# The run-in of an adaLN attention and MLP block: layer norm evicted unmodulated from two PSUM tensors, modulated in SBUF, K in two parts, later loads held back

## The chip, the cores and the metric

The kernel runs on one core of one Trainium2 chip. The metric is the device time of one execution in microseconds (us). The engines named below are PE (matrix multiply), ACT (ScalarE), DVE (VectorE), POOL (GpSimd) and SP, which here only issues transfers. A change of under 0.3% (2.35 us of 782.72) is about what a measurement of this kernel cannot tell from no change: the three runs shown lie 2.65 us apart.

## The reference

One block of 2048 tokens of width 512 with adaptive layer norm: six vectors come from a condition `c`, and modulate the input of a 32-head attention and of a GELU MLP.

```python
mod = (_silu(c) @ w_mod).reshape(c.shape[0], 6, 1, -1)
sa, ca, ga, sb, cb, gb = (mod[:, 0], mod[:, 1], ..., mod[:, 5])
h = _layernorm(x, axis=-1) * (1 + ca) + sa
x = x + ga * _A_ref(h, A_wqkv, A_wo)     # softmax(q k^T / 4) v per head of 16, then @ wo
h = _layernorm(x, axis=-1) * (1 + cb) + sb
x = x + gb * _B_ref(h, B_w1, B_b1, B_w2, B_b2)   # gelu(h @ w1 + b1) @ w2 + b2
```

Shapes: x (1, 2048, 512), wqkv (512, 1536), wo (512, 512), w1 (512, 1376), w2 (1376, 512), c (1, 512), w_mod (512, 3072), all bfloat16.

## The kernel before

**Tiling.** The tokens form four blocks of 512 (`QB`), each of four tiles of 128. A block is normalised (`layer_norm`: statistics by `stats`, `z` by `apply`), its `z` is transposed by PE through the identity into PSUM, and evicted into `blk` (also called h) while scale and shift `modA` are applied (`modulate`, lines 667 to 674). From h come K (`make_k`, into `kT`), V (`make_v`, into `VEB`) and Q (`make_q`, into `qm`), 128 columns (eight heads) at a time. `rs` holds variance plus EPS; no version here takes a root of it, so that step costs the same in both.

**Attention.** The work is cut into 32 runs: a block of queries and four heads (at the end, half a block of queries and eight heads). A run goes over 16 key tiles of 128 keys; one key tile has four units of 512 columns, one for each 32-row group of PE. There are two ways to take the exponential of a key tile:

- On ACT (`qk_a`): PE writes scores into the PSUM tensors `st3` (three units) and `st2` (two) in turn, ACT exponentiates 128x1536 or 128x1024 at once into `pt` (line 943).
- On DVE (`qk_d`): PE writes one unit into `ax`, DVE turns it into int16 bits `ph` (line 984), and four shifted copies `sh` are made of a whole key tile (lines 1000 and 1016; POOL takes some quarters of the last one, line 1022). PE then multiplies five readings with five scaled copies of V (`VEB`, `VX`).

Each run has 12 own key tiles for ACT and 4 shared ones that DVE takes; but where ACT runs out of own tiles before DVE has begun a shared one, ACT takes it (`next_tile`). Run 0 has one shared tile. So the number of tiles of each kind comes out of the order.

**Order.** The whole order of every engine is written by a planner (`class Plan`) when the kernel is built. Each operation has an engine, a planned duration, dependencies and a priority; the planner picks, step by step, the ready operation with the best priority, with a small term drawn from `SEEDS`, one number for each 12.5 us of planned time. Where PE would stand idle it puts in "heat": a 128x512 matmul on a zero tile `warm` (lines 466, 471 and 482), so that PE's clock stays up. On the chip each engine then goes through its list strictly in order.

**The run-in.** SP issues, in this order: x of block 0 in two halves (line 537), w_mod for the first modulation in two halves of 512 KB (line 547), 128 columns of the Q and K weights (line 557), x of block 1, 128 columns of the V weights, the rest of the three weights, x of blocks 2 and 3. The statistics of block 0 need x, the vector `modA` needs w_mod and the silu of c (`first_mod`, line 640, 32 matmuls, and an add on DVE, line 644). All 16 transposes of block 0 write into one PSUM tensor (`st3`), and DVE, ACT, DVE, DVE evict it with `modA` applied. Q and K of block 0 are written into a second PSUM tensor (`st2`), and evicted one after the other: Q half 0 on DVE, K on ACT, Q half 1 on DVE. In the profile each of these evictions begins only when the one before it has ended, on the other engine too. Then the first scores and exponentials follow. Blocks 1 to 3 are normalised between the exponentials of run 0.

**The end.** Blocks 0 to 2 get their output projection, second norm and MLP between the exponentials of the later runs; so does the first half of block 3. What follows the last exponential (`last_half`) is the second half of block 3.

Of the kernel before, what the change touches and what calls it, by code (L numbers as in the profile page):

```python
# [11 lines left out]
ACT = mybir.ActivationFunctionType  # L12
# [13 lines left out]
NPH = 5  # L26
# [37 lines left out]
SEEDS = (421, 872, 550, 568, 152, 412, 578, 215, 443, 644, 509, 573, 863, 621, 363, 765, 575, 623, 840, 572, 68, 536, 307, 910, 236, 857, 622, 26, 489, 196, 660, 895, 259, 934, 819, 96, 576, 477, 556, 345, 216, 481, 3, 336, 398, 276, 175, 772, 338, 592, 137, 10, 817, 569, 785, 228, 673, 798, 588, 808, 688, 864, 394, 776)  # L64
# [219 lines left out]
def kernel(  # L284
# [125 lines left out]

    APR = 32
# [128 lines left out]
    o_mod = op("NIL", None, 0.0, (), lat=0.0, prio=-2.0, acq=r_g)  # L540

# [3 lines left out]
    def load_mod(h):  # L545
        def go(o):
            nc.sync.dma_start(out=o_mod.tile[:, 4 * h:4 * h + 4, :].rearrange("p (j n) q -> p j (n q)", n=2),
                              in_=wm_src[:, 2 * h:2 * h + 2, 0:2 * D])
        return dma(go, (o_mod,), kb=420, prio=0.2 * h - 4.0)
    o_wm = {h: load_mod(h) for h in (0, 1)}  # L550
# [4 lines left out]
    def load_cols(i, lo, hi, prio):  # L555
        def go(o):
            nc.sync.dma_start(out=o_w[i].tile[:, :, lo:hi], in_=wq_src[:, :, i * D + lo:i * D + hi])
        return dma(go, (o_w[i],), kb=192 if lo == 0 else 340, prio=prio, n=1.2)
    o_w0 = {i: load_cols(i, 0, P, (-3.0, -2.8, -2.4)[i]) for i in range(3)}
    o_w1 = {}  # L560
    for b in range(1, NQ):
        o_x[b] = load_x(b)
        o_x[b].prio = 0.5 * b - 3.1
        o_w1[b - 1] = load_cols((1, 2, 0)[b - 1], P, D, 0.5 * b - 2.7)
# [73 lines left out]
    def first_mod(ps, j):  # L638
        for m in range(2 * NC):
            nc.tensor.matmul(out=ps[:, m:m + 1], lhsT=mod_cols(j)[:, m * P:(m + 1) * P], rhs=sc[:, j:j + 1],  # L640
                             start=(j == 0 and m == 0), stop=(j == NC - 1 and m == 2 * NC - 1))
    mm_A = chain([(lambda ps, j=j: first_mod(ps, j), 0.28) for j in range(NC)], [o_sc, o_mod], "modA", r_ax, [o_mod],
                 need=lambda j: o_wm[j // 2])
    o_mA = op("DVE", lambda o: nc.vector.tensor_tensor(out=modA, in0=mm_A.tile[:, 0:2 * NC], in1=plus, op=ALU.add),
              0.2, [mm_A] + o_plus, prio=0.0, rel=(mm_A,))

# [35 lines left out]
    def layer_norm(src, deps, mod, mod_dep, hold_z, alloc_h, engines, ps_res, kind, prio,  # L682
# [3 lines left out]
        new = kind == "in0"  # L686

        def stat(t):
            stats(ln, t, src(t))
            if new and t > 1:  # L690
                plus_eps(nc.vector, ln, 0 if t == 2 else t, t + 1)
        st = [op("DVE", lambda o, t=t: stat(t), 0.98 if new and t > 1 else 0.83, (deps[t], ln, after and after[t]),
                 prio=prio) for t in range(nt)]
        if new:
            rs = 3 * [op("POOL", lambda o: rstd(ln, 0, 3, True), 0.8, [st[2], o_mh], prio=0.0)]
            rs.append(op("POOL", lambda o: rstd(ln, 3, 4, True), 0.8, [st[3], o_mh], prio=0.0))
        else:
            rs = [x for i in range(nt // 2) for x in 2 * [op(
                "POOL", lambda o, i=i: rstd(ln, 2 * i, 2 * i + 2), 1.3, st[2 * i:2 * i + 2] + [o_mh], prio=0.0)]]
        z = op("NIL", None, 0.0, (rs[0], hold_z), lat=0.0, prio=0.0, acq=r_z)  # L700
        za = [op("DVE", lambda o, t=t: apply(ln, z, t, src(t)), 0.33, (z, rs[t]), prio=prio,
# [4 lines left out]
        if isinstance(ps_res, tuple):  # L706
            hold = op("NIL", None, 0.0, (), lat=0.0, prio=-1.0, acq=ps_res[0]) if new else None
            firsts = []
            parts = ((0, 1), (2,), (3,)) if hold is not None else ((0, 1), (2, 3))
            two = [None, None]  # L710
            for part in parts:
                for half in range(2):
                    def tr(o, half=half, part=part, prev=two[half]):
                        if prev is not None:
                            o.tile = prev.tile
                        elif hold is not None:
                            o.tile = hold.tile[:, half * QB:(half + 1) * QB]
                        o.ps = o.tile.bitcast(BF16)
                        for j in (2 * half, 2 * half + 1):
                            for t in part:  # L720
                                nc.tensor.transpose(
                                    out=o.ps[:, (j % 2) * QB + t * P:(j % 2) * QB + (t + 1) * P],
                                    in_=z.tile[:, t, j * P:(j + 1) * P], identity=ident)
                    one = op("PE", tr, len(part) * 2 * 0.0705, za[0:part[-1] + 1] + [o_id, two[half]],
                             lat=PEL, mode=("full", 0), kind=kind,
                             acq=None if two[half] is not None or hold is not None else ps_res[half], rel=(z,))
                    if two[half] is None:
                        firsts.append(one)
                    two[half] = one
            trs += two  # L730
            for half in range(2):
                one = two[half]
                for j in (2 * half, 2 * half + 1):
# [3 lines left out]
                        0.5 if e == "DVE" else 0.72, (one, mod_dep, h), prio=0.2, rel=(hold or firsts[half],)))  # L737
# [16 lines left out]

    o_h = {}
# [7 lines left out]
    def proj(b, w, cc, kind, acq, after=None, into=None):  # L763
        js = (0, 2, 1, 3) if b else (0, 1, 2, 3)
        return chain([(lambda ps, j=j: nc.tensor.matmul(  # L765
            out=ps[:, 0:QB] if into is None else into(), lhsT=w.tile[:, j, cc * P:(cc + 1) * P], rhs=o_h[b].tile[:, j, :],
            start=(j == js[0]), stop=(j == js[-1])), MM) for j in js],
# [807 lines left out]
```

## Time and profile before

| what | us |
|---|---|
| three runs | 780.78, 782.72, 783.43 |
| median | 782.72 |
| the profiled execution | 784.56 |
| its span, first to last instruction | 782.8 |
| first exponential begins, in the span | 17.06 |
| last exponential ends | 759.9 |
| exponentials on ACT (626) | 710.7 busy |

The span is counted from the first to the last instruction of the profiled execution; 1.8 us of its time lie outside it. "busy" is the time in which an engine executes. A group of instructions is named by line, engine, operation, output<-input. The chain of waits goes back from the last instruction, at each step to what released it.

### The profile page before, as it was taken

To read this page: it belongs to the slowest core of one execution; us is meant where nothing else is said; L and a number is where in the kernel's file an instruction comes from. 1 tells how busy PE (TensorE), PEld (TensorE's weight loads), DVE (VectorE), ACT (ScalarE), POOL (GpSimd) and SP (SyncE) were. 2 spreads that over 40 slices of the span, in tenths; PEclk is the share of its full clock that TensorE was granted. 3 is DMA by queue.
4 is the path that set the end of the run, shared out by engine and by line. 5 is a ranking of instruction groups with operands and counts; after the bars stand their busy time and mean duration, and the time that the engine had idled before them with its cause. 6 is when DMAs were issued, how large, how long until landed. Compare 5 with 4: busy or idle time off the path is not lost.

```text
span 782.8 us, 20830 instructions
## 1 busy us (share of the span) xinstructions
PE 729.6 (93%) x8267; PEld 270.1 (35%) x8349; DVE 720.3 (92%) x1270; ACT 751.2 (96%) x676; POOL 256.8 (33%) x497
## 2 busy tenths in 40 slices
PE   7889999999999989999998999999999999989997
PEld 3333333233332323333222233222334444434454
DVE  5879988999999999999999999999889999999984
ACT  2999999999999999999999999999999999999994
POOL 4432433433345345232323114333122142322330
PEclk9999999999999999999999999999999999999999
DMA  6043011000011101010101000100011001001100
GB/s 215 28 120 109 19 24 43 20 9 19 23 44 52 26 20 46 13 23 12 43 21 22 29 19 24 22 20 26 26 47 32 20 24 46 17 12 31 26 18 28
DMA packets 35091, 27.71 MB, mean 35 GB/s; under 512 B 17941, under 2 KB 28726, under 8 KB 34994
## 3 DMA queue, kind: packets, MB, share of 16 engines
q1 hardware_dynamic: 34986, 26.39, 12.2%
q8 instruction: 65, 1.06, 0.6%
q14 instruction: 32, 0.26, 0.1%
q10 hardware_dynamic: 8, 0.00, 0.0%
HBM read 20.77 MB, written 2.61 MB: 30 GB/s over the span
## 4 chain that ended last, share of the span: by engine, by line
PE 39%; ACT 33%; DVE 14%; issue 10%; DMA 3%; SPq 1%; DVEq 0%; ACTq 0%
ACT pt L943 31%; PE od L1082 13%; PE st L894 11%; DVE ph L984 5%; DVE sh L1000 4%; PE ax L1248 4%; PE ax L894 3%; PE ax L1309 2%; PE ax L765 2%; DMA dc<-dn 1%; DMA g<-in_w_mod_dram 1%; PE ax L812 1%; DVE sh L1016 1%; PE t L1419 1%; ACT g L1324 1%
## 5 line engine op out<-in xcount | busy, mean ns | idle before, releaser
L943 ACT ACTIVATE pt<-st 128x1536 bf16<-128x1536 f32 x626 | 710.7, 1325 | 5.6 <-PE st L894 4.5
L984 DVE TENSOR_SCALAR ph<-ax 128x512 int16<-128x512 f32 x484 | 316.9, 682 | 21.7 <-PE ax L894 18.7
L894 PE MATMUL st<-qm,kT 32*128 32x512 bf16 x1564 | 247.0, 385 | 24.0 <-ACT pt L943 16.5
L1000 DVE TENSOR_SCALAR sh<-ph 128x2048 int16<-128x2048 int16 x363 | 241.2, 694 | 3.2 <-PE od L1082 2.0
L1022 POOL TENSOR_TENSOR sh<-ph,pair_sh 128x256 int32<-128x256 int32 x234 | 142.6, 616 | 265.4 <-DVE sh L1000 188.8
L1082 PE MATMUL od<-sh,VX 128*32 128x512 bf16 (+1 forms) x2432 | 171.2, 340 | 4.1 <-DVE sh L1000 2.3
L894 PE MATMUL ax<-qm,kT 32*128 32x512 bf16 x484 | 162.9, 379 | 4.7 <-DVE ph L984 2.6
L894 PEld LDWEIGHTS <-kT 32*128 32x128 bf16 x2048 | 79.8, 91 | 240.3 <-issue 228.7
L1082 PE MATMUL od<-pt,VEB 128*32 128x512 bf16 (+1 forms) x1952 | 142.7, 341 | 0.0
L1082 PEld LDWEIGHTS <-VEB 128*32 128x32 bf16 x2560 | 62.4, 96 | 74.6 <-issue 61.6
L1082 PEld LDWEIGHTS <-VX 128*32 128x32 bf16 x2432 | 59.3, 95 | 82.9 <-issue 72.3
L1134 POOL TENSOR_TENSOR OT<-OD,RB 128x256 bf16<-128x256 f32 x38 | 28.4, 753 | 103.4 <-DVE sh L1000 51.5
L1016 DVE TENSOR_SCALAR sh<-ph 128x2048 int16<-128x2048 int16 (+3 forms) x85 | 48.3, 577 | 1.8 <-PE od L1082 1.7
L1082 PE MATMUL od<-ph,VEB 128*32 128x512 bf16 (+1 forms) x608 | 47.7, 340 | 0.5 <-DVE OD L1107 0.5
L1309 PE MATMUL ax<-blk,W 128*128 128x512 bf16 (+1 forms) x152 | 41.2, 351 | 2.1 <-issue 0.8
L1248 PE MATMUL ax<-w,g 128*128 128x512 bf16 x114 | 32.3, 381 | 2.5 <-ACT g L1319 1.0
L828 POOL TENSOR_SCALAR VX<-VEB 128x128 bf16<-128x128 bf16 x64 | 23.9, 373 | 31.0 <-DVE VEB L680 28.0
L765 PE MATMUL ax<-blk,w 128*128 128x512 bf16 x93 | 31.0, 382 | 2.8 <-issue 0.6
L1314 DVE TENSOR_SCALAR g<-ax,b1c 128x512 bf16<-128x512 f32 (+1 forms) x44 | 29.4, 677 | 1.2 <-PE ax L1309 0.7
L1134 POOL TENSOR_TENSOR OS<-OD,RB 128x256 bf16<-128x256 f32 x24 | 17.2, 729 | 31.5 <-DVE sh L1000 22.4
L651 DVE BATCH_NORM_STATS2 ln_s<-xb 128x6 f32<-128x512 bf16 x32 | 21.7, 679 | 1.1 <-DMA xb<-in_A_x_dram 1.0
L1248 PEld LDWEIGHTS <-g 128*128 128x128 bf16 x176 | 13.7, 97 | 24.4 <-issue 13.5
(110 smaller groups left out, 390.5 us busy)
## 6 DMA issues: line engine op xcount, KB each, us to landing
RB<-rn SPq DMA_DIRECT2D x124, 64.0 KB, 2.0
xb<-in_A_x_dram SPq DMA_DIRECT2D x7, 512.0 KB
g<-in_w_mod_dram SPq DMA_DIRECT2D x4, 512.0 KB, 6.6
out_dram<-o SPq DMA_DIRECT2D x16, 128.0 KB, 1.8
qm<-qs SPq DMA_DIRECT2D x120, 16.0 KB, 1.8
W<-in_B_w_dram SPq DMA_DIRECT2D x1, 1376.0 KB
w<-in_A_wqkv_dram SPq DMA_DIRECT2D x3, 384.0 KB, 6.6
xb<-in_w_mod_dram SPq DMA_DIRECT2D x2, 512.0 KB
```

Of the source, the lines that this page charges most:

```text
L765: return chain([(lambda ps, j=j: nc.tensor.matmul(out=ps[:, 0:QB] if into is None else into(), lhsT=w.tile[:, j, cc * P:(cc + 1) * P], rhs ...
L894: nc.tensor.matmul(out=o.tile[:, k * QB:(k + 1) * QB], lhsT=kT[cc][kb][rows, ko * P:(ko + 1) * P], rhs=qm.tile[rows, par, :] if hb is None ...
L943: nc.scalar.activation(out=e.tile[:, 0:len(got) * QB], in_=o.tile[:, 0:len(got) * QB], func=ACT.Exp, scale=ESC)
L984: nc.vector.tensor_scalar(out=ph.tile[:, o.row * QB:(o.row + 1) * QB], in0=o.tile, scalar1=PH_B, scalar2=0.0, op0=ALU.add, op1=ALU.max)
L1000: sh = op("DVE", lambda o, j=j: nc.vector.tensor_scalar(out=o.tile, in0=first.tile, scalar1=PH_SH[j], scalar2=None, op0=ALU.add), 0.6, es, ...
L1016: return nc.vector.tensor_scalar(out=sh.tile[:, at], in0=first.tile[:, at], scalar1=PH_SH[-1], scalar2=None, op0=ALU.add)
L1022: return nc.gpsimd.tensor_tensor(out=sh.tile[:, at].bitcast(I32), in0=first.tile[:, at].bitcast(I32), in1=pair_sh[:, 0:1].to_broadcast([P, ...
L1082: nc.tensor.matmul(out=o_od[r].tile[32 * i:32 * i + 32, n * HB:n * HB + w], lhsT=v_tile(kt, ph)[:, c0:c0 + 32], rhs=got[i][:, at:at + w], ...
L1134: two = beside(lambda c: nc.gpsimd.tensor_tensor(out=OT.tile[:, c], in0=OD.tile[:, c], in1=o5.tile[:, c], op=ALU.mult), (OT,), (OD, o5), f ...
L1248: nc.tensor.matmul(out=ps, lhsT=g[:, f, col:col + P], rhs=rhs, start=(f == 0), stop=(f == NF - 1))
L1309: mm = chain([(lambda ps, f=f, j=j, f0=f0: nc.tensor.matmul(out=ps[:, (f - f0) * N:(f - f0 + 1) * N], lhsT=W1[:, j, f * P:(f + 1) * P], rh ...
L1314: ev.append(op("DVE", lambda o, f=f, f0=f0, mm=mm: nc.vector.tensor_scalar(out=g.tile[:, f, 0:N], in0=mm.tile[:, (f - f0) * N:(f - f0 + 1) ...
```

## The change

- **Loads.** w_mod comes in four parts of 256 KB (one for each 128 rows j) in place of two. The first weight transfer waits until part 1 has landed (`behind`), and all transfers behind it on SP's queue wait with it: x of block 1, the V columns, the remaining columns, x of blocks 2 and 3.
- **Block 0** has a function of its own, `first_norm`. The transposes write into two PSUM tensors (halves j 0,1 into `st2`, j 2,3 into `st3`), three token tiles first, then the fourth. DVE copies from the one and ACT from the other into h, with no modulation. `modA` is computed beside that, its last quarter after the transposes. Then DVE modulates h in place in SBUF, four times 128x512.
- **Q and K of block 0** no longer share a tensor: Q goes into `st2`, K into `ax`.
- **K of blocks 0 and 1** (`split_k`, `SPLIT = 2`): columns 0 to 127 (one key tile) and 128 to 511 are multiplied and copied by ACT apart; the first key tile's scores wait for the first part alone (`o_k0`).
- **Blocks 1 to 3**: the addition of EPS moves from POOL to DVE (`soon`).
- **VX**: the scaled copies of V become four POOL operations in the planner in place of one of four instructions.
- **SEEDS**: 64 other numbers, so the planner breaks ties otherwise over the whole kernel.

```diff
-SEEDS = (421, 872, 550, ...)
+SEEDS = (738, 995, 770, ...)
...
+    def behind(i, load):
+        tc.add_manual_dep(load.ins, first[i].ins.name, mybir.DependencyInfo(
+            mybir.DependencyClass.Sync, mybir.DependencyReason.DATA), reason="order of loads")
...
-            nc.sync.dma_start(out=o_mod.tile[:, 4 * h:4 * h + 4, :].rearrange("p (j n) q -> p j (n q)", n=2),
-                              in_=wm_src[:, 2 * h:2 * h + 2, 0:2 * D])
-        return dma(go, (o_mod,), kb=420, prio=0.2 * h - 4.0)
-    o_wm = {h: load_mod(h) for h in (0, 1)}
+            first[j] = nc.sync.dma_start(out=mod_cols(j), in_=wm_src[:, j, 0:2 * D])
+        return dma(go, (o_mod,), kb=250, prio=0.2 * j - 4.6)
+    o_wm = {j: load_mod(j) for j in range(NC)}
...
+            if (lo, i) == (0, 0):
+                behind(1, got)
+        return dma(go, (o_w[i], o_wm[1]), kb=192 if lo == 0 else 340, prio=prio, n=1.2)
...
-            if new and t > 1:
-                plus_eps(nc.vector, ln, 0 if t == 2 else t, t + 1)
+            if soon and t % 2:
+                plus_eps(nc.vector, ln, t - 1, t + 1)
...
+    def first_norm(kind):
...
+        banks = [op("NIL", None, 0.0, (), lat=0.0, prio=-1.0, acq=r) for r in r_st[::-1]]
...
+        for lo, hi in ((0, 3), (3, 4)):
+            for half, e in enumerate(("DVE", "ACT")):
...
+                trs.append(op("PE", tr, 2 * (hi - lo) * 0.0705, za[lo:hi] + [banks[half], o_id], lat=PEL,
+                              mode=("full", 0), kind=kind, rel=(z,), prio=0.0))
+                ev.append(op(e, lambda o, half=half, e=e, lo=lo, hi=hi, rows=rows, view=view: copy(
+                    e, h.tile[:, 2 * half:2 * half + 2, lo * P:hi * P], rows(view())),
+                    (0.07 if e == "DVE" else 0.23) + (hi - lo) * 0.267, (trs[-1], h), prio=0.3, rel=(banks[half],)))
+        both = op("NIL", None, 0.0, [o_wm[NC - 1], trs[-1]], lat=0.0, prio=0.0)
+        mm = chain([(lambda ps, j=j: first_mod(ps, j), 0.55 / 2) for j in range(NC)], [o_sc, o_mod], "modA", r_ax,
+                   [o_mod], 1, lambda j: o_wm[j] if j < NC - 1 else both)
+        mA = op("DVE", lambda o: nc.vector.tensor_tensor(out=modA, in0=mm.tile[:, 0:2 * NC], in1=plus, op=ALU.add),
+                0.2, [mm, ev[2]] + o_plus, lat=0.03, prio=0.0, rel=(mm,))
+        done = [op("DVE", lambda o, j=j: modulate("DVE", h.tile[:, j, :], h.tile[:, j, :], modA, j), 0.21,
+                   [mA] + ev[j // 2::2], prio=0.05, port=True) for j in range(NC)]
...
+    def split_k(b, kind):
+        evs = []
+        for lo, hi in ((0, P), (P, QB)):
+            mm = chain([(lambda ps, j=j, lo=lo, hi=hi: nc.tensor.matmul(
+                out=ps[:, 0:hi - lo], lhsT=o_w[1].tile[:, j, 0:P], rhs=o_h[b].tile[:, j, lo:hi],
+                start=(j == 0), stop=(j == NC - 1)), MM * (hi - lo) / QB) for j in range(NC)],
+                [o_w[1], o_w0[1]], kind, r_ax, (o_h[b], o_w[1]), need=lambda j: o_hd[b][j])
+            evs.append(op("ACT", lambda o, mm=mm, lo=lo, hi=hi: copy("ACT", kT[0][b][:, lo:hi], mm.tile[:, 0:hi - lo]),
+                          0.2 + 0.3 * (hi - lo) / QB, (mm,), prio=0.3, rel=(mm,)))
...
-        return [evs[par or 0], o_k[(cc, kt // TPB)]], qm
+        return [evs[par or 0], o_k0[kt] if cc == 0 and kt in o_k0 else o_k[(cc, kt // TPB)]], qm
...
+        if b == 0:
+            o_h[b], o_hd[b], za, trs, o_mA = first_norm(kind)
...
+        if b < SPLIT:
+            split_k(b, kind)
+        else:
+            make_k(b, 0, kind, r_ax, "ACT")
```

## The prediction

> **What bounds the kernel now.** I read the table of busy time by stage first. Its columns are the stretch, then length, busy PE, PEld, DVE, ACT and POOL, the granted clock, the DMA share and GB/s.
>
> ```profile
> 10.00:20.00 10.00, 7.16 (x66) 3.59 (x63) 7.21 (x16) 4.30 (x5) 0.54 (x3) 0.94 0.59 183
> 20.00:30.00 10.00, 8.65 (x83) 3.97 (x83) 8.24 (x22) 8.11 (x9) 4.75 (x24) 0.89 0.17 54
> ...
> 100.00:400.00 300.00, 282.59 (x2963) 94.73 (x2987) 290.10 (x496) 298.95 (x265) 116.91 (x198) 0.99 0.11 28
> 400.00:700.00 300.00, 284.09 (x3314) 100.90 (x3352) 282.66 (x491) 298.63 (x253) 85.27 (x136) 1.00 0.09 25
> ```
>
> From 100 to 700 us ACT is busy 597.58 of 600 us. So the time is: the start of the first exponential, plus ACT's work, plus its stalls, plus what follows the last one. DVE is next with 572.76, so its load matters too. The chain of waits in order of time (start, us, what) shows the run-in:
>
> ```profile
> 2.11 7.59 DMA g<-in_w_mod_dram
> ...
> 10.54 1.15 PE st L721 x16
> 11.69 0.03 issue
> 11.72 0.55 DVE blk L673
> ...
> 12.29 0.79 ACT blk L670
> ...
> 13.11 0.55 DVE blk L673
> ...
> 15.20 0.76 DVE qm L791
> ...
> 15.98 0.59 ACT kT L678
> ```
>
> w_mod lands at 9.70, and then all is serial: transposes, three evictions in turn, Q and K, two more evictions in turn. The timeline of ACT (start, us, operation, idle before) gives the stalls after it:
>
> ```profile
> 17.06 4.62 ACT L943 ACTIVATE pt<-st 128x1536 bf16<-128x1536 f32 x4 [0.49 <-PE st L894]
> 22.49 2.37 ACT L943 ACTIVATE pt<-st 128x1536 bf16<-128x1536 f32 x2 [0.81 <-PE st L894]
> ...
> 26.79 0.59 ACT L678 CAST kT<-ax 128x512 bf16<-128x512 f32 x1 [0.60 <-PE ax L765]
> 27.86 3.71 ACT L943 ACTIVATE pt<-st 128x1536 bf16<-128x1536 f32 x3 [0.48 <-PE st L894]
> ...
> 41.72 2.37 ACT L943 ACTIVATE pt<-st 128x1536 bf16<-128x1536 f32 x2 [0.65 <-PE st L894]
> ```
>
> Between 17.06 and 45 ACT idles 0.81+0.60+0.48+0.65 = 2.54 us, from 60 to 760 another 2.5 (the stages above and their neighbours). Last, the timeline of PE:
>
> ```profile
> 3.95 1.39 PE L466 MATMUL ax<-warm 128*128 128x512 bf16 x3
> ...
> 6.27 0.60 PE L466 MATMUL ax<-warm 128*128 128x512 bf16 x2
> ...
> 7.23 0.17 PE L608 MATMUL ax<-ident,sr 4*128 4x4 bf16 x1
> ...
> 9.75 0.55 PE L640 MATMUL ax<-sc,g 128*128 128x1 bf16 x16 [0.89 <-DMA g<-in_w_mod_dram]
> ```
>
> The heats before 5.17 stand about 0.43 us apart, those after it 0.22. PE is through its first 19 heats only at 7.23; before the change that was covered by the load until 9.70.
>
> **The change, part by part.** I compared the instruction order of both programs, and put durations from the profiled execution on it.
>
> *First exponential.* PE's list in the changed program is: the same 19 heats, the small transpose, two heats, 24 small matmuls for three quarters of w_mod, then eight heats, 16 transposes, two heats, the last eight small matmuls, Q, K. Heats wait for nothing but hold what is behind them. 7.78 (end of two heats) + 24 x 0.029 (16 weight loads took 0.47) = 8.5; + 8 x 0.22 = 10.2; transposes as in the chain 1.15 = 11.4, against 11.69 now. So the earlier w_mod hardly moves the transposes: the heats stand where the load stood. `z` is no limit: DVE goes through four at 0.41 from 7.02, to 8.7. Then two heats 0.44, eight small matmuls and their latency 0.4, `modA` 0.17: 12.4. The copies to h lie beside this: DVE 384+384 columns (a 128x512 eviction took 0.54, so some 0.8) from about 10.9, then 0.35, done by 12.1; ACT on the other tensor some 0.85 and 0.4 from 11.3, done by 12.6, needed for the third modulation only. Four modulations in SBUF: the nearest row is `z`, same shape and two per-partition scalars, 0.73 for two, so 0.34 apart: 13.9. Q's last matmul 0.43: 14.3. DVE's list has the first statistics of block 1 in between (0.69+0.18), to 14.75; `qm` 0.75, scores 0.46, and ACT begins at about **16.0 in place of 17.06: -1.1**. K's casts (0.3 and 0.5, second one by about 15.7) stay covered. Ends: 15.2 (-1.9), if modulations cost what a 128x512 shift costs (0.33, the row with one scalar) and transposes run without gaps; 17.5 (+0.4), if the third quarter of w_mod lands only when the second half does now, at 9.70.
>
> *Transfers held back.* The weight transfers and x of blocks 1 to 3 go out after part 1 has landed. x and two quarters of w_mod are 1 MB; by the DMA answers for stretches of about 1 us, 1.05 MB have moved by 6 us (0.19, 0.27, 0.09, 0.19, 0.31), so the first weight transfer leaves at 6 to 7 instead of 2.62, and x of block 1 three transfers later, at about 8.2 instead of 3.85. At some 320 GB/s it is there by about 12, needed at 13.9; Q's columns are there by 10, needed at 12.8. I cost this at nothing; the cover is under 2 us, and each us by which x comes later than that delays `qm` by one.
>
> Whether holding them speeds w_mod at all is open. These are the DMA answers for 6 to 7 and 7 to 8 us:
>
> ```profile
> DMA packets 231, 0.33 MB, mean 333 GB/s; under 512 B 77, under 2 KB 77, under 8 KB 231
> ...
> DMA packets 708, 0.32 MB, mean 318 GB/s; under 512 B 636, under 2 KB 636, under 8 KB 708
> ```
>
> Packets under 512 B are the 128-column weights. They hardly flow before 7, while w_mod lands at 9.70: engines that are through with w_mod go ahead, and the slow ones share 320 GB/s with them. Without them the last parts come sooner, but not by half. The Trainium skill, page "DMA: Bandwidth & Descriptors", section "Queues, rings and completion order", says that each DMA engine consumes descriptors in ring order; by that rule alone transfers issued behind w_mod take nothing from it and holding them gains nothing. The trace agrees up to 7 us.
>
> The Trainium skill, page "TensorE: Matmul & The Clock Gate", section "Part 1: The HAM clock gate", says that the clock is released after a window of about 3.4 us that runs free, so that the number of slow matmuls varies between runs. Here ten heats were slow; by that rule the 7.23, now on the path, would move by up to a few times 0.2 us from run to run, which no single trace can show.
>
> *Stalls from the first exponential to 45 us.* The six exponentials over key block 0 last 6.99 us, so block 1 must follow in 7 us. DVE's chain (second `qm`, statistics, four `z`, two modulations) starts 1 us earlier, and loses the 0.55 wait for POOL's EPS but gains six small additions (0.15 each; one took 0.61 beside POOL's memsets). Block 1's second transposes stand behind five groups of value matmuls on PE. K of the first 128 columns is cast in about 0.3 instead of 0.6. I take 2.0 for 2.54: **-0.5**; ends -2.0 (only one stall is left) and +0.8.
>
> *ACT's own work.* The list has 314 exponentials of 1536 and 313 of 1024 columns, before 313, 312 and one of 512: four units more, one key tile that DVE takes no more (runs 1, 2 and 4 give up one each in the beginning, before 3 and 4 did). 710.7/1564 units = 0.454 each: **+1.8** (1.75 to 1.9). K of block 1 in two casts: **+0.2** (0.1 to 0.3).
>
> *Steady part.* DVE has 4 fewer `ph` (-2.7), but POOL takes 192 quarters in place of 234, so DVE's shifts cover 13,312 columns more, at 0.694 per 2048: +4.5. Run-in: two copies 1.1, four modulations 1.4, six additions 0.9, less three evictions 1.6. Sum +3.6 us on an engine busy 95% from 100 to 700. Other seeds put the whole order anew. ACT's 2.5 us of idle is near the floor, so I expect a little more: **+0.5**; ends -1.0 and +3.6 (all of DVE's load turned into stalls).
>
> *The end.* The order after the last exponential is the same; the last one has three units instead of one, which is in the count above: 0, ends -0.4 and +0.4.
>
> Sum: -1.1 - 0.5 + 1.8 + 0.2 + 0.5 = +0.9. The span becomes 783.7 and the profiled execution 785.5; that execution lies 1.84 above the median, so the median goes from 782.72 to **783.6**, within 0.3%. All ends together give -3.5 and +7.4.
>
> **Rivals.** *A: ACT is fed without a break.* The shorter K step, EPS on DVE and new seeds take its 5.0 us of idle after 17.06 down to 1.5: -3.5 in place of 0. With -1.1 and +2.0 that is -2.6: 780.1. For it: every stall in the run-in names PE's scores, behind K. Against: 42 fewer quarters on POOL, and the steady part has nearly nothing to give. It decides from 3.3 us saved.
>
> *B: DVE becomes the bound in the steady part (slower).* Its 3.6 us are paid as waits of PE for `sh` and then of ACT for scores: +0.9 - 0.5 + 3.6 = +4.0: 786.7. For it: DVE at 290 of 300 us in the first stage. Against: DVE still waits 18.7 us for scores in `ax`. It decides from about 2 us of the 3.6.
>
> *C: the held loads do not bring w_mod earlier.* The third quarter lands at 9.70, and eight heats and the transposes stand behind it: +1.5 on the forecast, +2.4: 785.1. For it: packets are mostly in order; against: slow engines share bandwidth after 7 us. The ring order that the Trainium skill's page "DMA: Bandwidth & Descriptors" states, in the section named above, speaks for this rival.
>
> **How the numbers follow.** The forecast, within the 0.3% that a measurement of this kernel can hardly tell from no change, 0.42; A 0.22, B 0.24, C 0.12. Hence faster 0.22, same 0.42, slower 0.36. The range leaves out what lies beyond A (all low ends, 779.2) and the joint high ends (790.1): 780.0 to 787.6.
>
> **What the changed profile would show.** Eight heats between the 24 small matmuls and the first transpose, transposes at 10.2; first exponential at 16.0 (A: no later; C: 17.5, with PE waiting for g before 9.7); modulations of 0.34 to 0.41; ACT's idle from there to 45 us near 2.0; 627 exponentials with some 712.5 us busy; ACT idle near 3 us from 60 to 760, and in case B 5 or more with PE waiting for `sh`. I am wrong if x of block 1 lands after 14, if the transposes come before 9.5, or if new seeds move ACT's stalls by more than 3 us.

## The result, and the profile after

The changed kernel takes 786.21 us in the median of 13 runs (783.61 to 788.03), the kernel before 781.85 us in 13 runs beside them (780.36 to 783.43). The ratio is 1.0054, with a 95% interval of 1.0040 to 1.0068: slower by half a per cent, 4.4 us. The profiled execution after took 787.85 us, with a span of 786.1. It lies near the top of its 13 runs, and the one before (784.56) above all of its own; so each term below is also read in a second execution, from the experiments.

The stages, after (length, then busy PE, PEld, DVE, ACT and POOL, granted clock, DMA share, GB/s):

```profile
10.00:20.00 10.00, 8.14 (x74) 4.33 (x73) 8.22 (x22) 5.91 (x8) 1.22 (x4) 1.00 0.65 211
20.00:30.00 10.00, 8.36 (x99) 4.47 (x96) 9.58 (x25) 9.02 (x11) 4.55 (x28) 1.00 0.33 106
100.00:400.00 300.00, 278.75 (x2926) 93.72 (x2949) 291.02 (x498) 296.64 (x263) 103.12 (x177) 0.99 0.10 28
400.00:700.00 300.00, 284.00 (x3332) 102.18 (x3365) 285.22 (x492) 296.33 (x251) 71.74 (x116) 1.00 0.10 25
```

From 10 to 30 us ACT is busier than before (14.93 against 12.41 us). From 100 to 700 it is less busy: 592.97 against 597.58. What the run-in gained was more than lost in the steady part, where the prediction expected a loss of only half a microsecond.

The chain of waits of the changed kernel in the run-in (start, us, what):

```profile
7.95 0.58 PE ax L647 x24
8.53 0.24 PE od L472
...
10.07 0.22 PE ax L467
10.29 0.35 PE st L776 x6
...
10.66 0.57 DVE blk L682
...
12.38 0.18 DVE modA L787
...
12.59 1.38 DVE blk L675 x4
13.97 0.61 DVE ln_s L653
...
14.79 0.65 DVE qm L835
```

The chain goes through no transfer any more. From 8.53 to 10.29 it goes through heats (lines 467 and 472): PE could have begun the transposes, and executes warm-up instead. The timeline of ACT (start, us, operation, idle before) has these stalls up to 45 us:

```profile
24.66 0.27 ACT L680 CAST kT<-ax 128x128 bf16<-128x128 f32 x1 [0.30 <-PE ax L812]
25.48 1.45 ACT L987 ACTIVATE pt<-st 128x1536 bf16<-128x1536 f32 x1 [0.56 <-PE st L938]
```

Then ACT's waits from 60 to 755 us, in total, times and the longest, after:

```profile
ACT pt L987 <- PE ax L938: 5.5, 6, 2.0
ACT pt L987 <- PE st L938: 1.0, 2, 0.7
```

and before:

```profile
ACT pt L943 <- PE st L894: 1.4, 3, 0.7
ACT pt L943 <- PE ax L894: 0.2, 1, 0.2
```

The stalls are few and long, six of them behind scores that PE writes for DVE (`ax`). The page's group for those scores (busy and mean, then PE's idle time before them) names a transfer after the change, where before it named `ph`. The first line is before, the second after:

```profile
L894 PE MATMUL ax<-qm,kT 32*128 32x512 bf16 x484 | 162.9, 379 | 4.7 <-DVE ph L984 2.6
L938 PE MATMUL ax<-qm,kT 32*128 32x512 bf16 x480 | 158.9, 379 | 9.0 <-DMA qm<-qs 3.7
```

The whole span can be cut into terms that add up: the first exponential's start F, ACT's idle time in three stretches, all of ACT's work from F to the end of the last exponential, and what follows it. One row is one profiled execution; "transpose" is the start of the small transpose of line 608 or 615, behind the first 19 heats, and part of F. What ACT idles between 755 and the end of its last exponential is in the third stretch (0.44 in e2, under 0.1 elsewhere).

| kernel | transpose | F | idle to 45 | 45 to 60 | from 60 | ACT's work | after the last | span |
|---|---|---|---|---|---|---|---|---|
| before | 7.23 | 17.06 | 2.53 | 0.87 | 2.49 | 736.91 | 22.94 | 782.8 |
| e6, before, loads held | 7.91 | 16.27 | 1.12 | 0.55 | 1.82 | 736.18 | 22.86 | 778.8 |
| e8, before, no draw | 7.87 | 16.80 | 1.66 | 0.49 | 2.82 | 742.05 | 23.08 | 786.9 |
| e2, before, seeds of after | 7.71 | 15.98 | 1.13 | 1.46 | 9.39 | 741.50 | 22.84 | 792.3 |
| after | 7.24 | 15.91 | 0.98 | 0.52 | 7.06 | 738.89 | 22.74 | 786.1 |
| e5, after, loads not held | 7.21 | 15.89 | 0.98 | 0.52 | 6.03 | 738.83 | 22.75 | 785.0 |
| e9, after, no draw | 7.77 | 16.44 | 0.98 | 0.52 | 4.88 | 742.44 | 22.94 | 788.2 |
| e1, after, seeds of before | 6.96 | 15.56 | 1.06 | 0.07 | 7.94 | 739.47 | 22.70 | 786.8 |
| e10, after, draws of before | 7.66 | 16.34 | 1.06 | 0.06 | 4.20 | 738.80 | 26.74 | 787.2 |
| e4, after, no heats | 6.67 | 14.45 | 0.98 | 0.52 | 2.83 | 738.45 | 22.77 | 780.0 |
| e12, no heats, Q rows on POOL | 7.97 | 14.91 | 4.01 | 0.52 | 4.34 | 739.19 | 23.03 | 786.0 |
| e11, after, Q rows on POOL | 7.82 | 16.49 | 0.98 | 0.52 | 5.55 | 739.36 | 23.00 | 785.9 |
| e7, e4 with Q rows ahead | 6.66 | 14.60 | 0.98 | 0.48 | 10.26 | 738.80 | 22.78 | 787.9 |
| e3, Q rows and w2 moved | 7.09 | 15.77 | 0.98 | 0.51 | 15.28 | 739.87 | 22.69 | 795.1 |

From before to after: -1.15 - 1.55 - 0.35 + 4.57 + 1.98 - 0.20 = +3.3. In this pair the third idle term decides. In other pairs it need not: e8 idles hardly more from 60 on than the kernel before (2.82 against 2.49), and its 4.1 us of longer span are ACT's work (+5.1), because ACT takes 631 exponentials there in place of 626 and DVE 472 units in place of 484.

### The profile page after: what moved, and what is told of

Its sections match the earlier page's. It is cut to its first block, busy times and chain, and to the rows that moved or that the text cites. A ratio compares the mean times of both kernels' runs of the same rounds, so it can differ in the third digit from the quotient of the medians.

```text
span 786.1 us, 20799 instructions
## 1 busy us (share of the span) xinstructions
PE 731.4 (93%) x8292; PEld 274.3 (35%) x8369; DVE 722.6 (92%) x1278; ACT 753.6 (96%) x680; POOL 225.5 (29%) x449
## 3 DMA queue, kind: packets, MB, share of 16 engines
q8 instruction: 65, 1.06, 0.6%
## 4 chain that ended last, share of the span: by engine, by line
PE 38%; ACT 30%; DVE 20%; issue 9%; DMA 2%; SPq 1%; DVEq 0%; POOL 0%; ACTq 0%; POOLq 0%
ACT pt L987 28%; PE od L1126 12%; PE st L938 10%; DVE ph L1028 8%; DVE sh L1044 6%; PE ax L1292 4%; PE ax L938 3%; PE ax L1353 2%; PE ax L803 1%; DMA qm<-qs 1%; DVE g L1358 1%; SPq L845 1%; PE ax L467 1%; DVE sh L1060 1%; DMA dc<-dn 1%
## 5 line engine op out<-in xcount | busy, mean ns | idle before, releaser
L987 ACT ACTIVATE pt<-st 128x1536 bf16<-128x1536 f32 x627 | 712.8, 1334 | 8.1 <-PE ax L938 5.5
L1028 DVE TENSOR_SCALAR ph<-ax 128x512 int16<-128x512 f32 x480 | 313.5, 683 | 26.7 <-PE ax L938 23.9
L1066 POOL TENSOR_TENSOR sh<-ph,pair_sh 128x256 int32<-128x256 int32 x192 | 116.1, 613 | 314.5 <-DVE sh L1044 161.5
L938 PEld LDWEIGHTS <-kT 32*128 32x128 bf16 x2048 | 82.1, 91 | 244.3 <-issue 232.1
L938 PE MATMUL ax<-qm,kT 32*128 32x512 bf16 x480 | 158.9, 379 | 9.0 <-DMA qm<-qs 3.7
L1126 PE MATMUL od<-pt,VEB 128*32 128x512 bf16 (+1 forms) x1956 | 144.6, 341 | 1.1 <-ACT pt L987 0.9
L1060 DVE TENSOR_SCALAR sh<-ph 128x2048 int16<-128x2048 int16 (+3 forms) x91 | 53.6, 593 | 0.1
```

Of the source, the lines that this page charges most:

```text
L938: nc.tensor.matmul(out=o.tile[:, k * QB:(k + 1) * QB], lhsT=kT[cc][kb][rows, ko * P:(ko + 1) * P], rhs=qm.tile[rows, par, :] if hb is None ...
L987: nc.scalar.activation(out=e.tile[:, 0:len(got) * QB], in_=o.tile[:, 0:len(got) * QB], func=ACT.Exp, scale=ESC)
L1028: nc.vector.tensor_scalar(out=ph.tile[:, o.row * QB:(o.row + 1) * QB], in0=o.tile, scalar1=PH_B, scalar2=0.0, op0=ALU.add, op1=ALU.max)
L1060: return nc.vector.tensor_scalar(out=sh.tile[:, at], in0=first.tile[:, at], scalar1=PH_SH[-1], scalar2=None, op0=ALU.add)
L1066: return nc.gpsimd.tensor_tensor(out=sh.tile[:, at].bitcast(I32), in0=first.tile[:, at].bitcast(I32), in1=pair_sh[:, 0:1].to_broadcast([P, ...
L1126: nc.tensor.matmul(out=o_od[r].tile[32 * i:32 * i + 32, n * HB:n * HB + w], lhsT=v_tile(kt, ph)[:, c0:c0 + 32], rhs=got[i][:, at:at + w], ...
```

## The experiments

Two theories stood at the beginning. **L** (the prediction's B): the front leaves DVE 3.6 us more work, which comes out as stalls. **O**: the front has little to do with it, and the loss lies in the order that the planner draws with the new `SEEDS`. One thing about the draw matters for every edit: for engines other than PE the random term also takes the line number of the operation's function. An edit that moves lines draws a new order for the whole kernel. So all the kernels here keep their number of lines, and where "the same order" is said, every instruction on the engines named stands where it stood. All of them compute the whole block.

### e1 and e2: the seeds exchanged

```diff
-SEEDS = (738, 995, 770, ...)     # e1, in the changed kernel
+SEEDS = (421, 872, 550, ...)
...
-SEEDS = (421, 872, 550, ...)     # e2, in the kernel before
+SEEDS = (738, 995, 770, ...)
```

> The changed kernel with the seeds of the kernel before, nothing else. Theory O (order): the 4.6 us that ACT idles more from 60 to 755 us (7.05 against 2.49) come from where the new draw of the order puts a few transfers and waits, not from the front's edits. Then another draw gives other stalls: ACT idle from 60 to 755 anywhere between 2 and 8, at other places, first exponential still at 15.9, time between 781 and 788. Theory L (load): DVE's extra work and POOL's fewer quarters, which the front brings, starve ACT. Then the idle stays at 6 or more and PE waits for sh, time 785 to 787.

> The kernel before with the seeds of the changed one, front as before. Theory O: a draw that was not chosen for this program, so ACT idles 4 to 8 us from 60 to 755 instead of 2.5, time 784 to 788 with the first exponential still at 17.06. Theory L: front as before, so the idle stays at 2 to 3.5 and the time within 1 us of the kernel before.

Measured: e1 789.89 us (785.79 to 795.01), ratio to before 1.0108 [1.0071, 1.0145]; e2 793.87 (791.39 to 795.10), 1.0151 [1.0130, 1.0173]. With the old front and the new seeds, the kernel is 12 us slower than before, with stalls like those of the changed kernel, at other places. The timeline of ACT in e2:

```profile
278.81 64.81 ACT L943 ACTIVATE pt<-st 128x1024 bf16<-128x1024 f32 x57 [1.27 <-PE ax L894]
...
588.30 2.37 ACT L943 ACTIVATE pt<-st 128x1536 bf16<-128x1536 f32 x2 [1.86 <-PE st L894]
591.57 2.36 ACT L943 ACTIVATE pt<-st 128x1536 bf16<-128x1536 f32 x2 [0.90 <-PE st L894]
595.01 1.45 ACT L943 ACTIVATE pt<-st 128x1536 bf16<-128x1536 f32 x1 [1.07 <-PE st L894]
```

So such stalls need no new front, and L is not needed to explain them. Each set of seeds is better in the kernel that it came with. Theory O had the direction and not the size: it gave 781 to 788 for e1 and 784 to 788 for e2, and both are slower than that. e2's first exponential came at 15.98, not at 17.06, because its w_mod was in time.

### e8 and e9: no draw at all

```diff
-SPREAD = 0.15
+SPREAD = 0.0       # e8: in the kernel before; e9: in the changed kernel
```

> The kernel before with no random term in the planner (the spread set to zero, so the seeds do nothing). Theory O: an unchosen order like that of e1 and e2, ACT idle from 60 to 755 of 4 to 12 us, time 785 to 795, with the same run-in. If the chosen seeds gave nothing, the time stays within 1.5 us of 781.5.

> The changed kernel with the draw's weight SPREAD at 0, so that its order is the planner's own, as in e8 for the kernel before (789.18). Both emit 631 exponentials on ScalarE and 472 on VectorE, so that this pair differs by the front and by what the front does to the same planner, and by no choice of seeds. Theory O (the front gains some 2 to 3 us before 45 us and keeps it; the half per cent lost is the order that the seeds drew for the rest): 785.5 to 788, that is 1 to 3.5 us under e8. Rival F (the front itself leaves the steady part worse, by VectorE's load or by its later buffers, whatever is drawn): 791 or more, that is 2 us or more above e8, with 4 us or more of ScalarE's idle time between 60 and 760 us beyond e8's 1.9.

Measured: e8 789.18 us (788.70 to 794.30), ratio to before 1.0104 [1.0079, 1.0130]; e9 789.77 (789.02 to 791.38), 1.0099 [1.0084, 1.0114]. Without a draw the two fronts cannot be told apart. The page's groups show that the work is then shared out nearly alike, in e8 first, then in e9:

```profile
L943 ACT ACTIVATE pt<-st 128x1536 bf16<-128x1536 f32 (+1 forms) x631 | 715.8, 1326 | 4.7 <-PE ax L894 1.7 <-PE st L894 1.5 <-PE od L1082 0.8
L1022 POOL TENSOR_TENSOR sh<-ph,pair_sh 128x256 int32<-128x256 int32 x189 | 114.5, 615 | 257.6 <-DVE sh L1000 163.2 <-DVE ph L984 51.1 <-PE ax L894 11.1
```

```profile
L987 ACT ACTIVATE pt<-st 128x1536 bf16<-128x1536 f32 (+1 forms) x631 | 716.4, 1324 | 5.9 <-PE st L938 2.6 <-PE ax L938 2.4 <-PE od L1126 0.4
L1066 POOL TENSOR_TENSOR sh<-ph,pair_sh 128x256 int32<-128x256 int32 x185 | 114.0, 625 | 264.3 <-DVE sh L1044 114.7 <-DVE ph L1028 100.3 <-DVE sh L1060 16.1
```

The 42 quarters that POOL lost in the change (234 to 192) thus need no new front: without a draw, the kernel before gives POOL 189. And DVE's load does rise with the front, from 565.78 us busy to 571.63 between 100 and 700 us (e8, e9), but no loss of time comes of it. This is where L falls. The forecast of O for e9, 1 to 3.5 us under e8, missed as well: the profiled executions show 1.0 us gained up to 45 us (16.80 + 1.66 against 16.44 + 0.98), and 2.1 more idle later. (The expectation's 1.9 for e8 is its idle time from 100 to 700 us; from 60 on it is 2.82.) These 2.1 us are no clean effect of the front either: in e9's execution the clock granted to PE was 0.50 from 589.9 to 596.7 us, and 1.96 us of ACT's idle time lie there; e8's execution kept 1.00 throughout this part. What the front is worth by itself is too small to be shown.

### e10: the draws of before in the changed kernel

```diff
-o.fn.__code__.co_firstlineno
+o.fn.__code__.co_firstlineno - shift(o.fn.__code__.co_firstlineno)   # line in the kernel before; SEEDS of before
```

> The changed kernel with the seeds of before and with the line numbers that enter the draw mapped back to those of the kernel before, so that every kind of work draws the numbers that it draws there; only the front and the times at which the planner asks differ. Theory O in its narrow form (the draws of before are good for this work, whatever front precedes them): 779 to 781, that is 1 to 3 us under before's 781.9. Theory O in its wide form (a draw is good only for the order it was chosen with, since every later choice hangs on the moments at which engines come free; with another front it is a new draw like any other): 785 to 793, as e1's 789.89. Rival F (the front costs the steady part): the same as the wide form, so that this run tells only the narrow form from the two.

Measured: 791.00 us (789.02 to 794.81), 1.0119 [1.0097, 1.0142]. The wide form of O holds: with another front, the same numbers draw another order. In the profiled execution the steady idle time is only 4.2 us, but 26.74 us follow the last exponential instead of 22.9, because the pieces behind it are ordered otherwise (ACT's timeline, start, us, operation, idle before):

```profile
772.78 1.51 ACT L672 ACTIVATE blk<-t,modB 128x128 bf16<-128x128 bf16 x4 [8.37 <-PE t L1451]
```

After the change that wait was 3.14. So the five orders that came about otherwise stand at 789.2 to 793.9 (e8, e2; e9, e1, e10), and the two kernels' own at 781.9 and 786.2. The draw is worth 7.3 us to the kernel before, against e8, and 3.6 us to the changed one, against e9; the difference, 3.8, is nearly the whole loss of 4.4. This only counts times; it doesn't say by which waits a good order gains. In the terms of the table e8 stands above the kernel before by ACT's work, e2 by both ACT's work (+4.6) and idle time (+6.9).

### e4: the eight heats left out

```diff
-        if o_warm.end is None or plan.now > plan.until:
+        if o_warm.end is None or plan.now > plan.until or quiet[0]:   # set from the third quarter of w_mod to the first transpose
```

> The changed kernel without the eight heats between the third quarter of w_mod and the transposes, all else in the same order. If the heats hold the run-in, as the prediction says: transposes at 8.7 (z is the limit) in place of 10.13, first exponential near 14.4 in place of 15.91, and the time falls by 1 to 1.5 us against the changed kernel. If another wait takes their place (x of block 1, which is needed 1.5 us sooner, or Q's columns): first exponential at 15.4 or later and less than 0.5 us.

Measured: 784.40 us (781.73 to 786.94), 1.0036 [1.0023, 1.0049], everything else in the same order. That is 1.8 us under the changed kernel in the median; the two intervals just overlap. F falls from 15.91 to 14.45. Of these 1.46 us, 0.57 are an earlier small transpose in this execution; the other 0.9 come because the transposes follow the small matmuls at once, until `z` is the limit (timeline of PE in e4):

```profile
6.67 0.17 PE L615 MATMUL ax<-ident,sr 4*128 4x4 bf16 x1
...
7.22 0.74 PE L647 MATMUL ax<-sc,g 128*128 128x1 bf16 x24
7.82 0.44 PE L776 MATMUL st<-ident,z 128*128 128x128 bf16 x2
8.58 0.73 PE L776 MATMUL st<-ident,z 128*128 128x128 bf16 x10 [0.32 <-DVE z L667]
```

The eight heats lay on the path. The same order of the later work stalls ACT for 2.83 us in this execution (the fastest of its 12), and for 7.06 in the one after the change (near its slowest): a good part of what a single profile shows as stalls moves from execution to execution.

Part of it moves with the clock granted to PE. e4's execution kept it at 1.00 from 60 to 755 us. After the change it fell once there (all engines, columns as in the table of stages):

```profile
239.00:240.60 1.60, 0.39 (x3) 0.19 (x3) 0.52 (x2) 1.60 (x3) 0.00 (x0) 1.00 0.00 0
240.60:244.00 3.40, 2.71 (x14) 0.50 (x14) 3.11 (x6) 1.42 (x2) 1.22 (x2) 0.51 0.09 23
244.00:248.00 4.00, 4.00 (x52) 1.18 (x51) 3.87 (x7) 3.80 (x4) 0.61 (x1) 0.99 0.26 65
```

PE has little to do for 1.6 us (0.39 busy), then its clock is halved for 3.4 us, and ACT's longest stall, 1.98 us, ends at 243.59 within that stretch. In e2 the clock was 0.50 from 586.4 to 596.6 us, and three of the four stalls shown above lie there; the fourth lies in another such stretch (275.7 to 279.1, 0.51). The times of whole executions follow the clock too: in the kernel before, 5 of the 62 executions beside the experiments had a mean clock of 1.000 and took 779.1 to 780.7 us, and 13 had 0.993 and took 782.4 to 785.0; e1, with 0.980 to 0.995, took 795.0 to 785.8. But the clock is not why the change lost: with a mean clock of 0.998 or more the changed kernel took 785.6 on average (8 of 13), the kernel before 780.9 (29 of 62). Whether a stall of PE always brings the fall, and what share of a stall the fall adds, no run separates.

### e5 and e6: holding the loads, taken away and added

```diff
-                behind(1, got)       # e5, in the changed kernel
+                pass
...
+            got = ...; (lo, i) == (0, 0) and tc.add_manual_dep(got.ins, mods[0].ins.name, ...)   # e6, in the kernel before
```

> The changed kernel with the one wait on SP's queue taken out, every engine's order the same: the Q columns and all behind them go out without waiting for w_mod's second part. If holding the loads brings w_mod earlier, the third quarter lands between 8.3 and 9.7 without it, PE waits for it inside the 24 small matmuls, the eight heats and the transposes slide by 0.5 to 1.9 us and the first exponential comes at 16.4 to 17.8; time up by 0.5 to 1.9 us against the changed kernel (787 to 788). If transfers are served in the order of their issue, the quarters land as before, the first exponential stays at 15.9 and the time at 786.

> The kernel before with that wait put in (the Q columns wait for the first half of w_mod), every engine's order the same. There the landing of w_mod ends the chain, so a speed-up shows in full: w_mod lands near 8 in place of 9.70, transposes 1.5 us sooner, first exponential at 15.5 and 1 to 1.5 us less (780.5). Served in the order of issue: landing within 0.3 us of 9.70 and no change; x of block 1 has 2 us of room, so a loss is not expected.

Measured: e5 784.85 us (783.50 to 788.54), 1.0042 [1.0024, 1.0059], against the changed kernel's 1.0054 [1.0040, 1.0068]; e6 781.26 (779.70 to 783.98), 0.9990 [0.9975, 1.0005]. No effect is shown in either: what was expected if holding speeds w_mod came in neither. In e5 the 24 small matmuls begin at 7.77 with no wait for w_mod, as with the hold (7.79). In the kernel before, PE waited for w_mod 1.25 us in its profiled execution, 0.53 in e8, and not at all in e2, none of which hold anything. The timeline of PE in e2:

```profile
8.27 0.95 PE L640 MATMUL ax<-sc,g 128*128 128x1 bf16 x32
```

### e3, e7, e11 and e12: the late Q rows

The stalls of the changed kernel have a face: PE waits for rows of Q (`qm<-qs`), of which eight small transfers go out for each block and head group, between the transfers of the softmax denominators (`dn<-OD`, `dc<-dn`, `rn<-dc`). SP's own timeline, after, and PE's behind it:

```profile
604.58 0.54 SPq L1159 DMA_DIRECT2D dc<-dn  x1
605.18 3.64 SPq L845 DMA_DIRECT2D qm<-qs  x4
608.86 0.58 SPq L1167 DMA_DIRECT2D rn<-dc  x1
```

```profile
610.16 0.37 PE L938 MATMUL ax<-qm,kT 32*128 32x512 bf16 x1 [1.46 <-DMA qm<-qs]
```

The longest stall of ACT (1.98 at 243.59) has another face, `dc<-dn` behind a load of MLP weights (1.78 us of DVE's time, from 238.30 to 240.08). It is this wait that leaves PE with little to do just before its clock falls at 240.6. In e5, with the same order on every engine, DVE's waits for `dc<-dn` come to 0.6 us in all, the clock stays at 1.00 from 235 to 248 us, and ACT doesn't stall there. I tried three mendings. e3 issues the eight Q rows together ahead of the denominators, and that load behind `dc<-dn`; e7, built on e4, moves two rows ahead of `rn<-dc`; e11 gives four of the eight rows to a queue of POOL, so that nothing of the denominators comes later.

```diff
-   rows = [... nc.sync.dma_start(out=qm.tile[at, p, :], ...) for i in range(16 * p, P, 32)]
+   # e3: the four transfers of p = 0 issue those of p = 1 too; the second w2 load goes out behind dc<-dn
+   # e7: the first two transfers of p = 1 issue two each
+   # e11, and e12 on top of e4:
+   rows = [... (nc.gpsimd if p else nc.sync).dma_start(out=qm.tile[at, p, :], ...) for i in range(16 * p, P, 32)]
```

> The changed kernel with two moves on SP's queue alone, the order of all other engines kept to the instruction: the eight small transfers that put a Q half in place (qm<-qs) are issued with the first four of them, so that no transfer of a run's denominators stands between them, and the second load of w2 is issued behind the read of a run's denominators (dc<-dn) instead of ahead of it. Theory O: PE's 3.7 us of waits for qm go and ACT's 1.98 us stall at 242 us, so ACT's idle from 60 to 755 falls from 7.05 to about 2 to 3 and the time by 4 us, to 782. Theory L: those were only the places where the shortage showed; ACT idles 5 or more elsewhere and the time falls by less than 1.5 us.

> The kernel of e4 (no eight heats) with one move on SP: the last two of the eight transfers of a Q half go out with the two before them, so they no longer stand behind the write-back of the denominators (rn<-dc), which waits for DVE; the reads of the denominators (dc<-dn) keep their place, unlike in e3. If the late last rows cause the waits for qm, PE's wait for qm falls from 1.9 to 4 us to under 1, ACT's idle in 500 to 700 us to under 1 and the time by 1 to 2.5 us against e4 (782 to 783.5). If the plan's order leaves no room there in any case, the wait moves to the denominators' way back (RB, the normalisation, and with it the next run) and the time stays or rises.

> The changed kernel (786.2) with the second four of each block's eight Q-row transfers (60 of the 120) issued by GpSimd on a queue of its own, each at the planner's place, instead of on SyncE behind the transfers of the denominators; the other engines' order is the same, and no transfer of the denominators is later than before. Theory Q (the late Q rows are the stall: TensorE's 3.7 us of waits for them make ScalarE's waits for an ax tile): those waits fall under 1 us, ScalarE's idle time between 60 and 755 us from 7.05 to about 3.5, 782.5 to 784. Rival V (the profile names the rows only because they come last; with them early the next work of the same place is late): the waits for Q rows fall and ScalarE's idle time stays at 5 to 8, 785 to 788. Rival G (GpSimd's issues delay the quarters of units that TensorE waits for): its waits for a GpSimd tile appear, 788 or more.

> The same without the eight heats ahead of the first transposes (e4 alone: 784.4). Theory Q: 780.5 to 782.5, so a kernel at or under the one before. Rivals V and G: as e4 or slower, 784 to 788. If the two edits add up, it stands 1.5 to 2 us under e11.

Measured: e3 799.98 us (796.95 to 802.86), 1.0235 [1.0210, 1.0260]. e7 790.44 (789.65 to 793.35), 1.0117 [1.0092, 1.0141], 6 us over e4. e11 787.46 (784.09 to 787.93), 1.0068 [1.0041, 1.0095]. e12 785.10 (783.36 to 787.76), 1.0055 [1.0034, 1.0076]. The gains that e3, e7 and theory Q had forecast came in none of them; e11 came out as rival V had it.

In e3 the denominators' read proves the more urgent transfer, and PE's waits for Q rows don't go either (4.2 us, against 3.7); e3 makes both of its moves at once, so that they are not told apart. DVE's wait for the read, from 60 to 755 us, after and then in e3:

```profile
DVE dc L1162 <- DMA dc<-dn: 3.5, 3, 1.8
```

```profile
DVE dc L1162 <- DMA dc<-dn: 9.2, 6, 2.2
```

With it ACT's idle time doubles from 7.06 to 15.28. In e7 PE's waits for Q rows rise from 1.9 (e4) to 5.2 us, though two rows go out earlier; why is not settled. After two of them (PE busy 1.82 of 4.20 and 4.33 of 6.50 us) the granted clock is 0.50 for 3.4 us each time. In e11 those waits fall from 3.7 to 1.7 and ACT's idle time from 7.06 to 5.55, and the time does not fall. Two stalls stay at the places where they were, and one of 0.44 grows to 1.43 (ACT's timeline in e11):

```profile
244.39 1.02 ACT L987 ACTIVATE pt<-st 128x1024 bf16<-128x1024 f32 x1 [1.77 <-PE ax L938]
...
346.85 70.23 ACT L987 ACTIVATE pt<-st 128x1536 bf16<-128x1536 f32 x62 [1.43 <-PE ax L938]
```

Both stalls shown here lie in stretches of half clock (0.50 from 241.8 to 245.2 and from 344.2 to 347.6). So the Q rows are one place where the order hurts, but not shown to be a cause that can be taken out by itself. e12 stands 2.4 us under e11, as e4 stands 1.8 under the changed kernel: leaving out the heats seems to pay both times, though the intervals overlap each time. No version ran faster than the kernel before; e6 is level with it.

## Why the prediction was right or wrong

The prediction said 783.6, range 780.0 to 787.6, and gave "slower" 0.36. The measured 786.2 lies in the range, but slower than the likeliest case had it. By its steps:

**First exponential, -1.1.** The number came out, 17.06 to 15.91, and so did its working in the main: transposes at 10.13 (10.2), `modA` done at 12.55 (12.4), four modulations in 1.38 (0.34 each), exponential at 15.91 (16.0). Two errors in between nearly cancel: the copies to h were cheaper (0.56 and 0.29 on DVE, against 0.8 and 0.35), and the last four transposes waited 0.31 us for the first of them, a wait that the sum did not have. The low end of 15.2 does not follow from its condition: 0.33 in place of 0.34 for four modulations is 0.04 us, not 0.8, and the 1.15 us for the transposes were without gaps already. And the gain itself was mostly the one execution's late w_mod. The four kernels with the old front start at 17.06, 15.98, 16.27 and 16.80 (mean 16.5); the seven with the new front and its heats at 15.56 to 16.49 (mean 16.1); 0.3 of this difference is that the small transpose happened to come earlier in the seven (mean 7.39 against 7.68). From the small transpose on, the new front with its heats takes 8.60 to 8.68 us in every execution. The old one takes 8.27 and 8.36 where w_mod is in time (e2, e6), 8.93 and 9.83 where it is late. So the new front is only better against a late load, and its own chain is longer by some 0.3; without the heats it takes 7.78 and 7.94, and 6.94 in e12, where `z` is no limit.

**Transfers held back, nothing.** Right, by e5 and e6. Rival C falls: no execution of the changed kernel waited for the third quarter. The Trainium skill ("DMA: Bandwidth & Descriptors", section "Queues, rings and completion order") states that each DMA engine consumes its descriptors in ring order. Both runs agree with what the prediction drew from that, that holding gains nothing.

**Stalls up to 45 us, -0.5.** Measured -1.55 in the pair of profiles, which is three times the forecast. But the mean of the three other kernels with the old front is 1.30, and 0.98 to 1.06 with the new front and its heats: -0.3. In the profiled execution before, the clock granted to PE was low there (columns as in the table of stages, PE alone):

```profile
17.00:20.00 3.00, 2.40 (x19) 0.79 0.00 0
20.00:25.00 5.00, 4.53 (x41) 0.78 0.31 96
```

I showed the line with a clock of 0.89 for 20 to 30 us and did not use it; the stalls that I wanted to shorten were partly those of a slow PE.

**ACT's own work, +1.8 and +0.2.** Right: +1.98 in ACT's whole work, 627 exponentials with 712.8 us busy (712.5 forecast).

**The end, 0.** -0.2.

**Steady part, +0.5, ends -1.0 and +3.6: this is the step that failed.** ACT's idle time went from 2.49 to 7.06 us, +4.6; in a second pair of executions (e6, e5) from 1.82 to 6.03, +4.2. The size moves from execution to execution: e4, with the same order behind the run-in, idles 2.83. An estimate from the medians gives as much as the pairs: 4.4 us slower, less 2.0 for ACT's work, plus what the front and its heats gained in the means over the rows of the table (0.5 in F, 0.6 up to 45 us, 0.45 from there to 60), is about 4. I took the end of that range from DVE's load, and treated the seeds as a matter of half a microsecond, since the idle time was "near the floor". A low idle time did not mean that the time could only be redrawn by so little: the two other orders in the kernel before stand 7.3 (e8) and 12.0 us (e2) above it, partly by idle time and partly by more work on ACT, and the three others in the changed one 3.6 to 4.8 us above that. Whether the old order is a rare one, so few cannot say. The condition "if new seeds move ACT's stalls by more than 3 us" is what happened.

**Rival B** gave 786.7, close to the result, for the wrong reason. A load of that size did come: from 100 to 700 us DVE is busy 576.24 us, against 572.76. But its mark was PE waiting for `sh`; from 60 to 755 us PE waited 1.8 us for it after, against 2.5 before. e2 shows such stalls, and e8 POOL's smaller share, without the new front; e9 carries the load and is level with e8. That the result lies so near 786.7 is luck. **Rival A** fell: the run-in did come close to its 1.5 us of idle (0.98 + 0.52 up to 60 us), and the steady part took it back.

**What stays open.** That the front is not the cause rests on e8 and e9, whose ratios differ by -0.0005 with intervals of 0.0015 to 0.0026 to either side; 0.0054 is beyond that. It is one order on each side, and a cost of the front of up to some 2 us (0.0025) is not excluded. The draw is named by exclusion: e10 did not bring the order of before back behind the new front. Which of PE's gaps are followed by a halved clock is open too. Which choices of the planner make one order good, and why e7's rows are waited for longer, is not settled. Fixing the order of the whole attention by hand behind either front was not tried.

## What to carry to other kernels

Where a drawn order happens to be a good one, any edit that changes the draw, be it the seeds, a time that the planner sees or here even a line number, puts that gain (7 to 12 us here) at stake before the edit's own gain (about 1 us) counts: compare with the draw off on both sides, and price the redraw as a term with its own range. Before you shorten a run-in, look at several executions: the wait that you remove may be one execution's late transfer or low clock; so look at the granted clock before you put a stall down to the work beside it. And when a load comes earlier, look at what the planner had put under its cover: filler work then stands on the path.

## What the runs showed of the hardware

**Slow heats move the whole run-in.** The small transpose behind the first 19 heats starts between 6.66 and 7.97 us over 14 profiled executions, and the new front follows it as one piece. The Trainium skill ("TensorE: Matmul & The Clock Gate", section "Part 1: The HAM clock gate") says that the number of slow matmuls varies with the phase of a free-running window. The traces agree: between 7 (e4, e7) and 13 (e6, e8, e11, e12) of the gaps between these heats are slow ones, mostly of 0.43 us against 0.22, which makes the spread of 1.3 us, larger than the gain that I forecast.

**The clock can fall again, in the run-in and later.** In the steady part one late transfer was followed by 3.4 us at half clock (0.39 of 1.6 us busy, then 0.51; see e4). In e12, with PE busy for 2.04 of 3 us just before, the clock granted fell to half from about 20 to 30 us, K and its scores came late, and ACT idled 4.01 us up to 45 us instead of 0.98. PE's stages in e12:

```profile
17.00:20.00 3.00, 2.04 (x17) 1.00 0.02 8
20.00:25.00 5.00, 3.96 (x32) 0.53 0.62 210
25.00:30.00 5.00, 5.00 (x34) 0.50 0.00 0
```

e4 has the same order of PE there and kept its clock at 1.00 in all three stretches, and e7 idled 0.98 too. So it happens in some executions; in the kernel before, with its own heats, it happened in a milder form. Whether leaving out heats makes it more frequent, three executions cannot say.

**Small transfers on one queue are not interchangeable.** Bringing 16 KB rows forward past an 8 KB read of denominators, and moving one weight load behind it, cost 14 us over the whole kernel (e3).
